# When a staged weight's conversion may begin during attention: two steps behind its load, and the late token-weight loads queued in group 5

## The chip, the core and the metric

The kernel runs on one core of a Trainium2 chip. Its time is the device time of one execution in microseconds (us), the median over runs. The core's engines work side by side, each on its own list of instructions in order: TensorE (PE in the profile; its weight loads are PEld), VectorE (DVE), ScalarE (ACT), GpSimd (POOL) and SyncE (SP), which here issues all DMA transfers.

## What is computed

Three layers follow each other, all in 32-bit precision, for 2 batches of 768 tokens with 512 features:

```python
# attention, 8 heads of 64: tokens attend only within their cluster
q_assign = argmax(q_n @ c_n);  k_assign = argmax(k_n @ c_n)
scores = scale * q @ k.T, where(q_assign == k_assign), else -1e9
attn = exp(scores - max);  out = (attn / (sum(attn) + 1e-9)) @ v
# token mixer
theta = x @ w_theta
y = w_tok_r @ (x * cos(theta)) + w_tok_i @ (x * sin(theta))
u = x + y;  x = u + relu(u @ w_ch)
# low-rank mixer and feed-forward
u = x + V.T (U.T x);  x = u + relu(u @ w_ch1) @ w_ch2
```

The weights come as 64-bit floats. Before a weight tile can be used it is converted to 32 bits and split into a high and a low part for TensorE.

## The kernel before, in words

**Stages.** `prologue` loads and packs the first heads, `attention` (L843) works through 8 groups of two heads (2 batches x 4 pairs), `mixer` does the rest. The whole order of instructions is written out by hand: what a Python call emits first stands first on its engine.

**A group of attention** has six steps, p = 0 to 5. In each step `scores_pair` (L304, L309) makes scores of the running group g on TensorE in three parts, and ScalarE their exponentials; `max_pair` (L251, L255) makes scores of the next group g+1 and VectorE three row reductions of them, so that a group has 18 reductions. After steps 2 and 5 `max_join` (L260) joins the maxima of one head, POOL splits them in two (`max_split`, L271, L272), and `max_rows` (L282 on TensorE, L285 copies on ScalarE) turns them into rows of the next group's operands. Step 5 of groups 1 to 6 ends in a *burst*: first background work is emitted, then P·V products of the whole group (L317) with `max_rows` of the next group's second head in their middle, the eviction `pv_out` (xT, L324) and the row sums (`sum_keys`, L346). In group 6 six of the twelve P·V pieces are left for group 7, which spreads them over its steps and makes no maxima.

**Operand copies.** For group g+2, `split_half` and `mask_rows` in steps 0 to 2 of group g split the raw heads and issue many small SBUF-to-SBUF copies on SyncE (L213). The value tile of group g+1 is loaded at the start of group g (`load_v`, L292).

**Weight conversion runs in the background of attention.** A `Convert` object is one tile of 128 x 768 (768 KB). Its pieces are: `load` (L390, SyncE, into one of three staging buffers `st`), `magnitude` (L399, ScalarE, out `cv`), `low` (a shift, L402, VectorE), `join` (L406, VectorE), then `hi` (L411, ScalarE, out `wh`) and `lo` (L415, POOL, out `wl`). The queues are: `conv_load` (not loaded yet), `conv_in` (loaded, at most three), `conv_do` (the pieces of the tile in hand) and `conv_after` (`hi` and `lo`). `conv_step` emits one piece. When a tile is joined, `last` emits the `magnitude` of the next tile in `conv_in` at once, whenever its load was issued:

```python
                    if conv_in:
                        conv_in[0].magnitude()
                    conv_start()
```

`fill` (L825) decides how many pieces a step gets: each step adds to a budget `owed`, 0.3 in most steps, 9.6 in the burst of groups 2 to 6, 2.5 in each step of group 7; other background items (`bg`) go first. `held[0]` is true during attention. Tiles of w_theta are queued in group 1, the first six of the token weights (wr and wi in turn, three of each) in group 2, and the other six, `late`, in group 6.

Of the kernel before, what the change touches and what calls it, by code (L numbers as in the profile page):

```python
# [25 lines left out]
NT = S // P  # L26
# [15 lines left out]
def tile_cluster_block(ctx: ExitStack, tc: tile.TileContext, qk, v, cent, wth, wr, wi, wch,  # L42
# [57 lines left out]
    def load_raw(g, i):  # L100
        t = slot(f"raw{g}_{i}")
        nc.sync.dma_start(out=t, in_=qk[g // NP, g % NP, i])
        raw[g, i] = t
# [154 lines left out]
    def max_join(g, h, eng=None):  # L258
        mx = small.tile([P, NT], F32, tag="mx", name="mx")
        nc.vector.tensor_reduce(mx, mx_t[g, h].rearrange("p (t n) -> p t n", n=2), axis=AX.X, op=ALU.max)  # L260
        mx_t[g, h] = mx
        max_split(g, h, eng or nc.gpsimd)
# [27 lines left out]
    def load_v(g):  # L290
        t = slot(f"v{g}", F32, [P, NT, P])
        nc.sync.dma_start(out=t, in_=v[g // NP, g % NP])  # L292
        v_t[g] = t
# [19 lines left out]
    def pv(g, kt, hf):  # L313
        if kt == 0 and hf == 0:
            pvt[g] = banks("pv", "pv")
        for r in range(0, P, 32):
            nc.tensor.matmul(out=pvt[g][hf][r:r + 32, :HALF], lhsT=v_t[g][:, kt, r:r + 32],  # L317
                             rhs=pt[g, r // 64, kt][:, cols(hf)],
                             start=(kt == 0), stop=(kt == NT - 1))

    def pv_out(g):
        xT[g] = slot(f"xT{g}")
        for hf in range(2):
            nc.scalar.activation(out=xT[g][:, cols(hf)], in_=pvt[g][hf][:, :HALF], func=AF.Copy)  # L324
        give("pv")
# [3 lines left out]
    def join_keys(g, h, eng):  # L329

        t = slot(f"pj{h}")
        eng.tensor_tensor(t, pt[g, h, 0], pt[g, h, 1], op=ALU.add)
        joined[g, h] = t
# [40 lines left out]
    def norm_x(g):  # L374
        nc.vector.tensor_tensor(xT[g], xT[g], rl.pop(g), op=ALU.mult)
# [42 lines left out]

    conv_load, conv_in, conv_do, conv_after = deque(), deque(), deque(), deque()
    held = [False]  # L420

    def conv_start():
        while conv_load and len(conv_in) < STAGED:
            c = conv_load.popleft()
            c.load()
            conv_in.append(c)

    def conv_step(n=1):

        for _ in range(n):  # L430
            if conv_after and not held[0]:
                conv_after.popleft()()
            if not conv_do:
                conv_start()
                if not conv_in:
                    return
                c = conv_in[0]

                def last(c=c):
                    c.join()  # L440
                    conv_in.popleft()
                    conv_after.extend([lambda f=f: f(c) for f in c.done])
                    if conv_in:
                        conv_in[0].magnitude()
                    conv_start()

                conv_do.extend((c.low, lambda: None, last))
                if c.t is None:
                    conv_do.appendleft(c.magnitude)
            conv_do.popleft()()  # L450
# [6 lines left out]
    def weigh_in(src, n, dst):  # L457
        return [Convert(src, n, i, keep_split(dst)) for i in range((n + S - 1) // S)]
# [57 lines left out]
    def split_x(b, t, eng=nc.vector):  # L516
        x = xT[b * NP + t]
        hi = slot(f"xh{t}", F32R)
        nc.scalar.activation(out=hi, in_=x, func=AF.Copy)
        lo = slot(f"xl{t}", F32R)  # L520
        eng.tensor_tensor(lo, x, f32(hi), op=ALU.subtract)
        xs[b, t] = (hi, lo)
# [320 lines left out]
    def attention():  # L843


        ORDER = [(0, 0), (0, 2), (0, 4), (1, 0), (1, 2), (1, 4)]
        BURST = (2, 5)
        pvq = deque()
        held[0] = True

        def next_pv():
            g, kt, hf = pvq.popleft()
            pv(g, kt, hf)
            if kt == NT - 1 and hf:
                pv_out(g)

        for g in range(NG):
            nxt = g + 1 < NG
            if g == 1:
                conv_load.extend(weigh_in(wth, NP * DM, wth_t))  # L860
                conv_start()
            if nxt:
                load_v(g + 1)
            if g < 2:
                bg.extend(assign.pop(g + 2))
            if g + 3 < NG:
                for i in range(2):
                    load_raw(g + 3, i)
            if g == 2:
                tok = [c for p in zip(weigh_in(wr, NT * S, wr_t), weigh_in(wi, NT * S, wi_t)) for c in p]  # L870
                conv_load.extend(tok[:6])
                conv_start()
                late = tok[6:]
            if g == 6:
                conv_load.extend(late)
                conv_start()
            if not nxt:
                for t in range(NP):
                    bg.append((1., lambda t=t: split_x(0, t, nc.gpsimd)))
            order = [(1, 0), None, (1, 2), None, (1, 4), None] if g == 0 else ORDER  # L880
            for p in range(NT):
                ready = len(pvq)
                if order[p]:
                    h, a = order[p]
                    scores_pair(g, h, a)
                    if h:
                        pvq.extend((g, kt, hf) for kt in (a, a + 1) for hf in range(2))
                if g == 0 and p < 2:
                    mask_direct(1, p, nc.scalar if p else nc.vector)
                if nxt:  # L890
                    max_pair(g + 1, p // 3, 2 * p % 6)
                    if p % 3 == 2:
                        max_join(g + 1, p // 3)

                while conv_after:
                    conv_after.popleft()()
                if p in ((1, 4) if g < 4 or not nxt else (2, 4)):
                    join_keys(g, p // 4, nc.gpsimd if g < 4 else nc.vector)
                    if 4 <= g < NG - 1 and p == 4:
                        owed[0] -= .95  # L900
                if p < 2 and g + 2 < NG:
                    split_half(g + 2, p)
                if p == (3 if g < 2 else 2) and g + 2 < NG:
                    mask_rows(g + 2)
                long = 0 < g < NG - 1 and p == 5
                if long:
                    if g + 3 < NG:
                        (_, sims), *items = assign_items(g + 3)
                        sims()
                        bg.extend(items)  # L910
                    max_rows(g + 1, 0)
                if g > 0 and p == 5:
                    bg.appendleft((.95, lambda: norm_x(g - 1)))
                    bg.appendleft((.97, lambda: spread(g - 1)))
                fill(2.5 if not nxt else .3 if p not in BURST or (g > 1 and p == 2) else 9.6 if g > 1 else 4.8)
                if not nxt:
                    for _ in range(min(ready, (2, 2, 2, 0, 4, 4)[p])):
                        next_pv()
                    if p == 5:
                        sum_keys(g, 0)  # L920
                elif long:
                    ready = len(pvq) - (6 if g == NG - 2 else 0)
                    for n in range(ready):
                        if n == ready // 2:
                            max_rows(g + 1, 1)
                        next_pv()
                    sum_keys(g, 0, NT)
                elif p == 2 and g < 2:
                    if g > 0:
                        max_rows(g, 1)  # L930
                        sum_keys(g - 1, 1)
                    for _ in range(min(ready, 6)):
                        next_pv()
                elif p == 5:
                    max_rows(g + 1, 0)
                    for _ in range(min(ready, 6)):
                        next_pv()
                    sum_keys(g, 0)
                    (_, sims), *assign[g + 3] = assign_items(g + 3)
                    sims()  # L940
                if g > 0 and p == 2:
                    row_sums(g - 1)
            while bg:
                fill(.5)
            while g and conv_after:
                conv_after.popleft()()
        held[0] = False
        while len(pvq) > 1:
            next_pv()
        nc.scalar.activation(out=warm, in_=warm, func=AF.Sin)  # L950
        next_pv()
        sum_keys(NG - 1, 1)
# [286 lines left out]
```

## Time and profile before

| | us |
|---|---|
| median of 3 runs | 675.95 |
| lowest to highest run | 675.38 to 677.36 |
| the profiled execution's own time | 675.26 |
| its span, from the first to the last instruction | 673.5 |
| TensorE busy in the span | 658.3 (98%) |
| VectorE busy | 462.3 (69%) |
| ScalarE busy | 358.3 (53%) |
| POOL busy | 313.1 (46%) |
| granted TensorE clock, mean | 0.997 of full speed |

The page sums each engine over the whole span, so that stages with different limits lie in one number. For the groups of attention one reads the table by stage (busy time of each engine in a stretch of time) and the timeline, whose rows give an instruction's start, how long it or a run of equal ones took, and in brackets how long the engine had been idle before it and what ended that. In this execution group 5 begins at 155.01 us, group 6 at 179.42, group 7 at 206.49 and the mixer at 231.45 (the first scores or theta product of each).

### The profile page before, as it was taken

To read this page: it belongs to the slowest core of one execution; us is meant where nothing else is said; L and a number is where in the kernel's file an instruction comes from. 1 tells how busy PE (TensorE), PEld (TensorE's weight loads), DVE (VectorE), ACT (ScalarE), POOL (GpSimd) and SP (SyncE) were. 2 spreads that over 40 slices of the span, in tenths; PEclk is the share of its full clock that TensorE was granted. 3 is DMA by queue.
4 is the path that set the end of the run, shared out by engine and by line. 5 is a ranking of instruction groups with operands and counts; after the bars stand their busy time and mean duration, and the time that the engine had idled before them with its cause. 6 is when DMAs were issued, how large, how long until landed. Compare 5 with 4: busy or idle time off the path is not lost.

```text
span 673.5 us, 11931 instructions
## 1 busy us (share of the span) xinstructions
PE 658.3 (98%) x4559; PEld 579.8 (86%) x4560; DVE 462.3 (69%) x795; ACT 358.3 (53%) x726; POOL 313.1 (46%) x325
## 2 busy tenths in 40 slices
PE   8899999999889999999999999999999999999998
PEld 3567777777565599999999998899999999999997
DVE  7888698797688575547375547758876576776554
ACT  8648477667388554455464445634553444543231
POOL 9445156324048532114233144967666564746221
PEclk9899999999999999999999999999999999999999
DMA  6868668766604211003101221012221222110013
GB/s 201 216 146 261 173 143 254 218 165 172 219 0 150 87 48 33 1 0 110 48 24 33 77 65 48 26 38 80 73 84 35 76 79 79 32 32 2 0 48 141
DMA packets 21786, 62.57 MB, mean 93 GB/s; under 512 B 4224, under 2 KB 7296, under 8 KB 21728
## 3 DMA queue, kind: packets, MB, share of 16 engines
q1 hardware_dynamic: 21728, 61.80, 31.7%
q8 instruction: 36, 0.59, 0.4%
q14 instruction: 22, 0.18, 0.1%
HBM read 40.35 MB, written 3.15 MB: 65 GB/s over the span
## 4 chain that ended last, share of the span: by engine, by line
PE 89%; DVE 6%; ACT 2%; DMA 1%; SPq 1%; issue 1%; POOL 0%; POOLq 0%; DVEq 0%; ACTq 0%
PE acc L810 17%; PE q L758 15%; PE y L576 15%; PE st L304 8%; PE pv L317 8%; PE h L596 5%; PE th L534 5%; PE smax L251 3%; DVE mx L255 3%; PE l L346 3%; PE g L712 3%; PE acc L731 2%; DMA st<-in_wi_dram 1%; PE sims L121 1%; PE tp L614 1%; SPq L213 1%
## 5 line engine op out<-in xcount | busy, mean ns | idle before, releaser
L810 PE MATMUL acc<-g,wh 128*128 128x384 f32 x448 | 113.6, 334 | 0.0
L772 POOL TENSOR_TENSOR g<-sum,g 128x384 fp32r<-128x384 f32 x56 | 61.9, 1107 | 83.4 <-ACT g L771 83.4
L255 DVE TENSOR_REDUCE mx<-smax 128x1 f32<-128x512 f32 x144 | 89.1, 680 | 14.5 <-PE smax L251 14.5
L766 DVE TENSOR_TENSOR xT<-acc,xT 128x384 f32<-128x384 f32 x112 | 61.9, 555 | 46.3 <-PE acc L810 46.2
L309 ACT ACTIVATE p<-st 128x512 f32<-128x512 f32 x192 | 80.2, 530 | 25.1 <-PE st L304 24.6
L576 PE MATMUL y<-wh,z 128*128 128x384 f32 x384 | 87.6, 340 | 0.3 <-ACT z L554 0.3
L304 PE MATMUL st<-qp,kp 128*128 128x256 f32 (+1 forms) x384 | 79.4, 348 | 2.4 <-ACT p L309 1.5
L810 PEld LDWEIGHTS acc<-g,wh 128*128 128x128 f32 x448 | 80.7, 188 | 0.1
L415 POOL TENSOR_TENSOR wl<-cv,wh 128x768 fp32r<-128x768 f32 (+1 forms) x31 | 56.2, 1819 | 49.2 <-ACT wh L411 35.4
L810 PE MATMUL acc<-g,wl 128*128 128x384 f32 x224 | 74.8, 334 | 0.0
L304 PEld LDWEIGHTS st<-qp,kp 128*128 128x128 f32 x384 | 57.8, 191 | 19.5 <-issue 7.2
L770 ACT ACTIVATE sum<-sum 128x384 f32<-128x384 f32 x56 | 29.3, 523 | 82.3 <-DVE sum L766 82.3
L766 DVE TENSOR_TENSOR sum<-q,sum 128x384 f32<-128x384 f32 x98 | 53.0, 553 | 24.3 <-PE q L758 20.8
L576 PEld LDWEIGHTS y<-wh,z 128*128 128x128 f32 x384 | 66.9, 188 | 0.5 <-ACT z L554 0.5
L317 PE MATMUL pv<-p,v 128*32 128x384 f32 x768 | 66.6, 487 | 0.0
L560 POOL TENSOR_TENSOR z<-tht,z 128x256 fp32r<-128x256 f32 x24 | 18.2, 756 | 91.7 <-ACT z L554 91.6
L317 PEld LDWEIGHTS pv<-p,v 128*32 128x32 f32 x768 | 38.9, 110 | 18.7 <-issue 8.2
L406 DVE SCALAR_TENSOR_TENSOR cv<-cv,st 128x768 int32<-128x768 int32 (+3 forms) x47 | 49.5, 1054 | 0.8
L251 PE MATMUL smax<-kp,qp 128*128 128x512 f32 x192 | 44.6, 349 | 4.6 <-ACT qp L285 2.0
L576 PE MATMUL y<-wl,z 128*128 128x384 f32 x192 | 48.8, 335 | 0.0
L251 PEld LDWEIGHTS smax<-kp,qp 128*128 128x128 f32 x192 | 32.8, 191 | 15.3 <-issue 4.3
L193 POOL TENSOR_TENSOR lo<-raw,hi 128x768 fp32r<-128x768 f32 x16 | 29.3, 1838 | 35.4 <-ACT hi L188 24.2
(177 smaller groups left out, 1440.8 us busy)
## 6 DMA issues: line engine op xcount, KB each, us to landing
st<-in_w_dram SPq DMA_DIRECT2D x17, 512.0 KB, 3.6
st<-in_w_dram SPq DMA_DIRECT2D x10, 768.0 KB, 4.2
raw<-in_qk_dram SPq DMA_DIRECT2D x16, 384.0 KB, 5.0
qp<-hi SPq DMA_DIRECT2D x26, 192.0 KB, 3.1
st<-in_wr_dram SPq DMA_DIRECT2D x6, 768.0 KB, 4.3
st<-in_wi_dram SPq DMA_DIRECT2D x6, 768.0 KB, 5.8
kp<-hi SPq DMA_DIRECT2D x32, 96.0 KB, 3.1
qp<-lo SPq DMA_DIRECT2D x32, 96.0 KB, 2.7
```

Source lines behind the costliest of these rows:

```text
L251: nc.tensor.matmul(out=ps[:, c:c + w], lhsT=qp[s, h, 0][:, (a + j) * P:(a + j + 1) * P], rhs=kp[s, h, 0][:, k0:k0 + w], start=True, stop=True)
L255: nc.vector.tensor_reduce(mx_t[g, h][:, o:o + n], ps.rearrange("p (n w) -> p n w", n=n), axis=AX.X, op=ALU.max)
L304: nc.tensor.matmul(out=ps[:, c:c + n], lhsT=kp[s, h, w][:, (a + j) * P:(a + j + 1) * P], rhs=qp[s, h, w][:, q0:q0 + n], start=(w == 0), st ...
L309: nc.scalar.activation(out=pt[g, h, a + j][:, q0:q0 + n], in_=ps[:, c:c + n], func=AF.Exp, scale=float(D) ** -0.5)
L317: nc.tensor.matmul(out=pvt[g][hf][r:r + 32, :HALF], lhsT=v_t[g][:, kt, r:r + 32], rhs=pt[g, r // 64, kt][:, cols(hf)], start=(kt == 0), st ...
L406: nc.vector.scalar_tensor_tensor(t, t, 3, self.lw, op0=ALU.logical_shift_left, op1=ALU.bitwise_or)
L415: nc.gpsimd.tensor_tensor(t[:, :c.w], c.t, f32(c.hi[:, :c.w]), op=ALU.subtract)
L576: nc.tensor.matmul(out=yps[u, j][hf][:, :HALF], lhsT=lhs, rhs=w[st][e][:, hf * HALF:(hf + 1) * HALF], start=(st == 0 and n == 0), stop=(st ...
L758: nc.tensor.matmul(out=ps[:, :HALF], lhsT=w[a][:, j * P:(j + 1) * P], rhs=u_block(self.b, y, e, j), start=(n == 0), stop=(n == 5))
L766: nc.vector.tensor_tensor(out, ps[:, :HALF], x, op=ALU.add)
L772: nc.gpsimd.tensor_tensor(t[:, 1], r, f32(t[:, 0]), op=ALU.subtract)
L810: nc.tensor.matmul(out=ps[:, :HALF], lhsT=wv[a], rhs=self.g[i, hf][:, x], start=(m == 0), stop=(m == 5))
```

## The change

A counter `clock` holds the number of the running attention step, 6g + p. A load notes it. During attention a tile's `magnitude` may only be emitted when at least two steps have passed since its load was emitted, both in `last`, where the next tile's `magnitude` follows a join, and in `conv_step`, where a new tile is taken in hand. After attention nothing is asked. And the six late tiles are queued at the start of group 5 instead of group 6.

```diff
+    clock = [0]
+
+    def landed(c):
+
+        return not held[0] or clock[0] - c.at > 1
...
             c = conv_load.popleft()
             c.load()
+            c.at = clock[0]
             conv_in.append(c)
...
-                if not conv_in:
+                if not conv_in or not (conv_in[0].t is not None or landed(conv_in[0])):
                     return
...
-                    if conv_in:
+                    if conv_in and landed(conv_in[0]):
                         conv_in[0].magnitude()
...
-            if g == 6:
+            if g == 5:
                 conv_load.extend(late)
                 conv_start()
...
                 ready = len(pvq)
+                clock[0] = NT * g + p
```

What it moves is seen in the engines' orders. On ScalarE, at the end of group 5 and the first steps of group 6 (qp<-mrow are the copies of the maxima, cv<-st a `magnitude`, xT the eviction, wh a `hi`, p<-st the exponentials), before:

```order
L285 ACTIVATE qp_86<-mrow 2x384 x2
L399 ACTIVATE cv<-st 128x768 x3
L285 ACTIVATE qp_90<-mrow 2x384 x2
L324 ACTIVATE xT_2511<-pv 128x384 x2
L411 ACTIVATE wh<-cv 128x768 x3
L309 ACTIVATE p_2555<-st 128x512
```

and after:

```order
L285 ACTIVATE qp_86<-mrow 2x384 x2
L399 ACTIVATE cv<-st 128x768 x2
L285 ACTIVATE qp_90<-mrow 2x384 x2
L324 ACTIVATE xT_2513<-pv 128x384 x2
L411 ACTIVATE wh<-cv 128x768 x3
...
L309 ACTIVATE p_2582<-st 128x512
L399 ACTIVATE cv<-st 128x768
L309 ACTIVATE p_2610<-st 128x512
```

The third `magnitude` of the burst (the third tile of wi) now stands behind the exponentials of step 1 of group 6. In group 7 the pieces of the fourth wi tile and those behind it stand up to a step later; its three `magnitude` and three `hi` stay within the group.

On VectorE, among the reductions of group 6's steps 0 to 2 (mx<-smax) and in its burst (rb and xT<-xT,rb are the normalisation, st<-st a `low`, cv<-cv,st a `join`), before:

```order
L255 TENSOR_REDUCE mx_2572<-smax 128x1
L402 TENSOR_SCALAR st<-st 128x768
L255 TENSOR_REDUCE mx_2572<-smax 128x1
L255 TENSOR_REDUCE mx_2572<-smax 128x2
...
L371 STREAM_TRANSPOSE rb<-rl 128x768
L375 TENSOR_TENSOR xT_2511<-xT_2511,rb 128x768
L406 SCALAR_TENSOR_TENSOR cv<-cv,st 128x768
```

and after:

```order
L255 TENSOR_REDUCE mx_2570<-smax 128x1 x2
L255 TENSOR_REDUCE mx_2570<-smax 128x2
...
L371 STREAM_TRANSPOSE rb<-rl 128x768
L375 TENSOR_TENSOR xT_2513<-xT_2513,rb 128x768
L402 TENSOR_SCALAR st<-st 128x768
L406 SCALAR_TENSOR_TENSOR cv<-cv,st 128x768
```

The `low` has left the reductions and stands in the burst, directly ahead of its `join`.

On SyncE, behind the last operand copies for group 7 (kp<-oh), before:

```order
L213 DMA kp_99<-oh 16x384
L390 DMA st<-in_wi_dram 128x1536
L292 DMA v_2549<-in_v_dram 128x768
L390 DMA st<-in_wr_dram 128x1536
L390 DMA st<-in_wi_dram 128x1536
```

and after:

```order
L213 DMA kp_99<-oh 16x384
L390 DMA st<-in_wi_dram 128x1536
L390 DMA st<-in_wr_dram 128x1536
L390 DMA st<-in_wi_dram 128x1536
L292 DMA v_2551<-in_v_dram 128x768
```

The value tile of group 7 has moved behind the fourth tiles of wr and wi. TensorE's order is the same in both.

## Rows read from the trace of the kernel before

**Rows 1.** The page, part 1: engine, busy us, share of the span, instructions
```profile
PE 658.3 (98%) x4559; PEld 579.8 (86%) x4560; DVE 462.3 (69%) x795; ACT 358.3 (53%) x726; POOL 313.1 (46%) x325
```
**Rows 2.** Table by stage, groups 5, 6, 7: stretch, length, busy us, clock, DMA
```profile
155.01:179.42 24.41, 24.41 (x221) 18.08 (x222) 19.54 (x33) 14.36 (x31) 6.67 (x14) 1.00 0.64 166
179.42:206.49 27.07, 22.24 (x173) 15.22 (x173) 20.92 (x32) 19.81 (x40) 10.81 (x17) 1.00 0.27 102
206.49:231.45 24.96, 24.96 (x234) 12.43 (x233) 18.13 (x15) 20.01 (x40) 20.48 (x16) 1.00 0.41 130
```
**Rows 3.** Timeline, SyncE's queue: start us, us, engine line operation tiles
```profile
175.63 0.53 SPq L390 DMA_DIRECT2D st<-in_wi_dram  x1
176.26 0.38 SPq L292 DMA_DIRECT2D v<-in_v_dram  x1
176.73 0.38 SPq L390 DMA_DIRECT2D st<-in_wr_dram  x1
177.21 0.50 SPq L390 DMA_DIRECT2D st<-in_wi_dram  x1
```
**Rows 4.** Chain of waits (start, us, what); line 390's landings, 150 to 225 us
```profile
175.63 5.49 DMA st<-in_wi_dram
...
DMA to landing us min/median/max: 4.2/4.4/8.9
```
**Rows 5.** Timeline, ScalarE, groups 5 and 6
```profile
157.94 1.66 ACT L309 ACTIVATE p<-st 128x512 f32<-128x512 f32 x4
...
169.35 1.79 ACT L399 ACTIVATE cv<-st 128x768 f32<-128x768 f32 x2
181.21 0.89 ACT L399 ACTIVATE cv<-st 128x768 f32<-128x768 f32 x1 [10.07 <-DMA st<-in_wi_dram]
182.12 0.97 ACT L285 ACTIVATE qp<-mrow 2x384 fp32r<-2x384 f32 x2
```
**Rows 6.** Timeline, TensorE, groups 5 and 6
```profile
167.96 0.23 PE L282 MATMUL mrow<-identb,m 128*2 128x128 bf16 x2
...
183.14 1.01 PE L251 MATMUL smax<-kp,qp 128*128 128x256 f32 x3 [1.98 <-ACT qp L285]
...
186.72 0.73 PE L304 MATMUL st<-qp,kp 128*128 128x512 f32 x2 [1.48 <-ACT p L309]
...
197.46 0.23 PE L282 MATMUL mrow<-identb,m 128*2 128x128 bf16 x2
...
200.99 0.27 PE L282 MATMUL mrow<-identb,m 128*2 128x128 bf16 x3 [1.26 <-POOL m L272]
```
**Rows 7.** Timeline, VectorE: reductions and last joins of groups 5 and 6
```profile
156.86 1.89 DVE L255 TENSOR_REDUCE mx<-smax 128x1 f32<-128x512 f32 x3 [1.22 <-PE smax L251]
...
170.64 0.17 DVE L260 TENSOR_REDUCE mx<-mx 128x6 f32<-128x12 f32 x1
...
181.20 0.69 DVE L255 TENSOR_REDUCE mx<-smax 128x1 f32<-128x512 f32 x1 [1.22 <-PE smax L251]
183.68 1.29 DVE L255 TENSOR_REDUCE mx<-smax 128x2 f32<-128x512 f32 x2 [1.79 <-PE smax L251]
187.81 1.89 DVE L255 TENSOR_REDUCE mx<-smax 128x1 f32<-128x512 f32 x3 [2.84 <-PE smax L251]
189.62 1.02 DVE L402 TENSOR_SCALAR st<-st 128x768 int32<-128x768 int32 x1
...
200.13 0.17 DVE L260 TENSOR_REDUCE mx<-mx 128x6 f32<-128x12 f32 x1
```
**Rows 8.** Timeline, the burst of group 6 and what follows: VectorE, ScalarE
```profile
202.96 0.57 DVE L402 TENSOR_SCALAR st<-st 128x768 int32<-128x768 int32 x1
...
207.20 1.64 ACT L309 ACTIVATE p<-st 128x512 f32<-128x512 f32 x4 [1.67 <-PE st L304]
```
**Rows 9.** Timeline, end of group 7: last exponentials, P·V that reads them
```profile
222.20 1.81 ACT L309 ACTIVATE p<-st 128x512 f32<-128x512 f32 x4
...
226.75 2.76 PE L317 MATMUL pv<-p,v 128*32 128x384 f32 x32
```

## The prediction

> **What bounds the kernel now.** I read the page first: TensorE is busy for 658.3 of 673.5 us [rows 1], so only a place where it stands still, or works at another engine's pace, can give time. Then the table by stage, cut at the starts of the attention groups [rows 2]. Group 5 takes 24.41 us with TensorE busy throughout. Group 6 takes 27.07 us with TensorE busy for 22.24, although its program holds less TensorE work than group 5's (half of the P·V products of its end are left for the last group). Group 7 has no idle time again. So the change can gain in group 6.
>
> The timeline shows the cause. In the burst at the end of group 5 ScalarE converts three staged weights in a row, ahead of the copies of the second row of maxima. The first two run at 169.35 us; the third, the third tile of wi, waits 10.07 us for its transfer [rows 5]. SyncE has issued that transfer only at 175.63 us, because the operand copies of group 7 stand ahead of it [rows 3], and it lands 5.49 us later [rows 4]. Behind the waiting conversion stand, on ScalarE, the two copies of maxima (182.12 us), the eviction of xT, three weight splits and the exponentials of group 6. TensorE goes on with P·V and row sums, which need nothing from ScalarE, and then stands: 1.98 us until the copies of maxima free a bank, 1.48 us for an exponential, and 1.26 us later for the split of the maxima on POOL [rows 6].
>
> The third of these waits is the one that sets the price. VectorE must make 18 row maxima in a group; their join, POOL's split and the second row of maxima on TensorE end the group. In group 5 this runs from 156.86 to 170.81 us (the last join starts at 170.64 and takes 0.17), 13.95 us. In group 6 it runs from 181.20 to 200.30 us, 19.10 us: VectorE stands 1.79 and 2.84 us because TensorE delivers no products, and a weight's shift (1.02 us at 189.62) lies between the maxima [rows 7].
>
> **The change, part by part.**
>
> *The rule of two steps.* Only one conversion is put off: the third of wi, loaded in step 5 of group 5, may begin in step 1 of group 6. It leaves ScalarE's queue in the burst and comes back behind the exponentials of step 1. No instruction is added or lost. I take the wait of 10.07 us as gone. What does that give?
> - By TensorE's own idle rows, 1.98 + 1.48 = 3.46 us: the lower value.
> - By VectorE's chain, 19.10 − 13.95 = 5.15 us. The check: the waits 1.79 + 2.84 = 4.63 and the shift of 1.02 make 5.65; group 5's chain has some half a microsecond of short waits of its own, which come back.
>
> I take 5.15, because the chain also ends last after the change: the first maximum stays at 181.20 us (its product is out before the stall), so the last join ends at 181.20 + 13.95 = 195.15 us. TensorE reaches the first row of maxima 12.95 us after the group's start in group 5 (167.96 − 155.01), thus at 179.42 + 12.95 = 192.37 us here, and has P·V for 2.27 us (in group 6 from 197.46 to 200.99 − 1.26 = 199.73) [rows 6]: it is ready at 194.6 us and waits for VectorE and POOL once more. So the 1.26 us stays, about as long, and all that the chain gains TensorE gains. From the last join to group 7's first scores it takes 206.49 − 200.30 = 6.19 us as before; group 7 begins at 201.3 instead of 206.49 us.
>
> *The conversion in step 1 of group 6.* ScalarE spends 0.9 us more there (181.21 took 0.89 [rows 5]). In group 5 a split of the same size lies behind the exponentials of steps 0 and 1 and costs TensorE nothing, so I cost it at nothing. Its cover is ScalarE's idle time: 14.36 of 24.41 us busy in group 5 [rows 2].
>
> *The shift of wi's low bits* leaves VectorE's maxima and stands in the burst of group 6 behind the normalisation. There a shift costs 0.57 us alone [rows 8]. The two weight splits on ScalarE behind it come 0.6 us later; ScalarE has 1.67 us in hand before the exponentials of group 7 [rows 8]. Cost nothing; without that cover 0.6 us.
>
> *The late loads, one group earlier.* Without them the queue holds the same transfers; with them wr's and wi's fourth tiles are issued directly behind the third wi, and the value tile of group 7 goes behind both. On SyncE that moves it from 176.26 to about 177.2 us [rows 3]; it is read from 206 us on, or 201 after the gain, and lands long before. The fourth wi waits for a staging buffer whose join runs in the same burst. The next load behind these is only issued in the burst of group 6. Cost nothing.
>
> *The last group.* Steps 1 to 5 there hold three conversions and three weight splits on ScalarE; these now begin in step 2. Total work is the same (20.01 of 24.96 us busy [rows 2]). The step that loses is 5: two more pieces of about 1 us stand ahead of its exponentials in steps 3 and 4, while step 2 lost two, so I estimate them 1.1 us late. They end at 222.20 + 1.81 = 224.0 us before; P·V that reads them begins at 226.75 us [rows 9]. 1.1 is under 2.7. Cost nothing; bound, if ScalarE were late by all six pieces of about 1 us, 6 − 2.7 = 3.3 us.
>
> **Sum.** 675.26 (the profiled execution) − 5.15 = 670.1 us. That execution lies 0.7 us below the median of the three runs, 675.95; I state the forecast for the median: 675.95 − 5.15 = **670.8 us**.
>
> **Rivals.**
> - *A. Only the visible idle goes*, 3.46 us: 672.5. It would be so if VectorE's chain in group 6 is slow by itself and not by the stall. For it: the chain also bounds after the change, and POOL's three weight splits now run earlier, beside it. Against it: the rows of group 5, with the same 18 maxima and no stall, and VectorE's two waits named as waits for TensorE [rows 7].
> - *B. The wait moves to step 1 of group 6*, so the change does not do what it says. The rule counts steps of the program, not landings, and the load is issued by SyncE long after its place in the program. The step's exponentials end in group 5 at 159.43 us or 4.42 us after the group's start (157.94 + 1.66, less the overlap of 0.17) [rows 5]; in group 6 that is 183.8 us. The transfer landed at 181.1 us, so it has 2.7 us in hand. The same three transfers follow it, but now the two of 768 KB stand ahead of the value tile of 384 KB. If it shares evenly with the next two, 5.49 × 2304/1920 = 6.6 us (768 KB three times against 768, 384 and 768), landing at 182.2, still in time; with the longest landing of this line, 8.9 us [rows 4], at 184.5, a wait of 0.7 us: 671.5 at most, as the banks hold products for more than that. The Trainium skill, DMA: Bandwidth & Descriptors, section Queues, rings and completion order, states that each engine takes descriptors in ring order, so what is queued behind a transfer would not slow it. By that rule alone B would have no chance; the landing of 5.49 us beside a median of 4.4 [rows 4] speaks against trusting it.
> - *C. Slower than before*, by B's mechanism at a larger size: ScalarE stands in step 1, where no burst of P·V covers TensorE. Each microsecond beyond 183.8 then costs up to one; the gain of 5.15 is used up and another 2.03 lost once the tile lands after 191.0 us, which is 15.4 us after its issue. No landing of this line comes near. Time from there: over 678.0.
> - *D. The last group gives it back*, by up to 3.3 us from ScalarE's lateness: 672 to 674.1.
> - *E. No change*, 676: group 7's start is held by something that the trace does not show as last, such as the operand copies. Against it: these are issued before 175.6 us.
>
> **How the numbers follow.** 0.3% of 675.95 is 2.03 us, about what a measurement can tell from no change. Forecast (gain of 4.3 to 5.7) 0.72; A 0.14; B 0.05; D 0.04; E 0.03; C 0.02. The first four are faster by more than 2.03: 0.95; E is the same: 0.03; C slower: 0.02. The range reaches at the low end to a gain of 5.65 from the profiled execution, 669.6, less 0.2 for scatter: 669.4. At the high end it takes in A and B, 672.5, and half a microsecond of scatter: 673.0. The forecast, A and B hold 0.91 of the chance; scatter and misjudged terms take the rest down to 0.8.
>
> **What would show it.** In the profile after, ScalarE's wait for wi's transfer is gone or under 1 us; TensorE's two waits of 1.98 and 1.48 us are gone and one of about 1.2 us for POOL's split stays; the last join of group 6 ends at about 195.2 us, 13.9 to 14.0 after the first maximum; group 6 takes about 21.9 us and group 7 about 25.0. The forecast is wrong if group 6 keeps over 23.5 us, if a wait for a transfer appears behind the exponentials of its step 1, or if group 7 or the stage after it grows by more than a microsecond.

## The result and the profile after

The changed kernel takes 670.93 us (median of 6 runs, 670.34 to 672.43); the kernel before, run beside it, 676.83 us (6 runs, 675.38 to 678.64). The ratio is 0.9915, with a 95% interval of 0.9896 to 0.9935: faster by some 5.8 us (the medians differ by 5.90). The forecast was 670.8 us, and its gain 5.15. The profiled execution took 670.64 us, its span 668.9.

The table by stage, cut where the groups begin in this trace (stretch, length, busy us of PE, PEld, DVE, ACT, POOL, then clock and DMA), for groups 5, 6, 7:

```profile
155.60:179.94 24.34, 24.34 (x221) 18.02 (x221) 19.52 (x32) 18.50 (x38) 8.52 (x16) 1.00 0.64 167
179.94:201.93 21.99, 20.73 (x173) 15.26 (x173) 19.96 (x32) 15.89 (x33) 8.36 (x15) 1.00 0.31 115
201.93:226.87 24.94, 24.94 (x233) 12.45 (x233) 17.18 (x15) 20.17 (x40) 20.98 (x17) 1.00 0.42 139
```

One cut of [rows 2] has to be set right first. In all of these stretches the cut lies 0.07 us behind the row with the group's first scores; only group 6 of the kernel before was cut 0.14 us behind its row. Cut like the others, at 179.35, groups 5 and 6 of the kernel before read:

```profile
179.28 1.66 PE L304 MATMUL st<-qp,kp 128*128 128x512 f32 x8
...
206.42 1.68 PE L304 MATMUL st<-qp,kp 128*128 128x512 f32 x8
```

```profile
155.01:179.35 24.34, 24.34 (x221) 18.01 (x221) 19.52 (x32) 14.36 (x31) 6.67 (x14) 1.00 0.64 165
179.35:206.49 27.14, 22.31 (x173) 15.29 (x173) 20.93 (x32) 19.81 (x40) 10.81 (x17) 1.00 0.27 103
```

So group 6 fell from 27.14 to 21.99 us, by 5.15; the groups beside it moved by 0.02 us at most. The mixer takes the rest of the span, 668.9 − 226.87 = 442.03 us against 673.5 − 231.45 = 442.05 before. So the whole difference of the two traces lies in group 6, but for 0.6 us by which this execution began group 5 later (155.60 against 155.01).

ScalarE in the timeline, burst of group 5 and first steps of group 6, answers to [rows 5]:

```profile
169.94 1.79 ACT L399 ACTIVATE cv<-st 128x768 f32<-128x768 f32 x2
172.88 0.97 ACT L285 ACTIVATE qp<-mrow 2x384 fp32r<-2x384 f32 x2 [1.15 <-PE mrow L282]
...
182.72 1.64 ACT L309 ACTIVATE p<-st 128x512 f32<-128x512 f32 x4 [0.44 <-PE st L304]
184.22 0.91 ACT L399 ACTIVATE cv<-st 128x768 f32<-128x768 f32 x1
185.00 1.67 ACT L309 ACTIVATE p<-st 128x512 f32<-128x512 f32 x4
```

Two conversions run in the burst, and the copies of the maxima follow as soon as TensorE has their product. The third conversion runs at 184.22 us, with no idle time before it. VectorE and TensorE answer to [rows 7] and [rows 6]:

```profile
181.79 1.89 DVE L255 TENSOR_REDUCE mx<-smax 128x1 f32<-128x512 f32 x3 [1.22 <-PE smax L251]
...
195.57 0.17 DVE L260 TENSOR_REDUCE mx<-mx 128x6 f32<-128x12 f32 x1
```

```profile
192.90 0.23 PE L282 MATMUL mrow<-identb,m 128*2 128x128 bf16 x2
...
196.43 0.27 PE L282 MATMUL mrow<-identb,m 128*2 128x128 bf16 x3 [1.25 <-POOL m L272]
```

From the first maximum to the end of the last join VectorE's chain takes 195.57 + 0.17 − 181.79 = 13.95 us, the time of group 5 before, in place of 19.10. TensorE's waits of 1.98 and 1.48 us are gone; the one for POOL's split is still there, 1.25 against 1.26 us. And SyncE's queue, answering to [rows 3]:

```profile
176.25 0.53 SPq L390 DMA_DIRECT2D st<-in_wi_dram  x1
176.87 0.38 SPq L390 DMA_DIRECT2D st<-in_wr_dram  x1
177.34 0.38 SPq L390 DMA_DIRECT2D st<-in_wi_dram  x1
177.82 0.93 SPq L292 DMA_DIRECT2D v<-in_v_dram  x1
```

### The profile page after: what moved, and what is told of

It is laid out like the page before. It is cut to its first block, busy times and chain, and to the rows that moved or that the text cites. A ratio compares the mean times of both kernels' runs of the same rounds, so it can differ in the third digit from the quotient of the medians.

```text
span 668.9 us, 11928 instructions
## 1 busy us (share of the span) xinstructions
PE 657.9 (98%) x4559; PEld 580.5 (87%) x4560; DVE 460.8 (69%) x795; ACT 358.9 (54%) x726; POOL 313.1 (47%) x325
## 4 chain that ended last, share of the span: by engine, by line
PE 92%; DVE 5%; ACT 2%; DMA 1%; issue 0%; SPq 0%; POOL 0%; POOLq 0%; DVEq 0%
PE acc L816 17%; PE q L764 15%; PE y L582 15%; PE st L304 9%; PE pv L317 9%; PE h L602 5%; PE th L540 5%; PE smax L251 4%; PE l L346 4%; DVE mx L255 3%; PE g L718 3%; PE acc L737 3%; PE tp L620 1%; PE th L544 1%; PE sims L121 1%; DMA raw<-in_qk_dram 1%
```

## The experiments

The theories. **S**: ScalarE's wait of 10 us for one transfer is the cause, and SyncE's queue the reason for it. **V**: VectorE's chain sets the end of group 6, so a delay is priced by what it does to that chain. Rivals: **A**, only the visible idle time of TensorE counts; **Q**, the earlier loads bring the gain. The length of group 6 is read from each run's table by stage.

| kernel | group 6, us | ratio to before (95% interval) |
|---|---|---|
| before | 27.14 | 1 |
| changed | 21.99 | 0.9915 (0.9896 to 0.9935) |
| loads alone | 27.13 | 1.000 (0.9984 to 1.0016) |
| rule alone | 21.99 | 0.9936 (0.9918 to 0.9954) |
| rule alone, again | 22.00 | 0.993 (0.9913 to 0.9947) |
| changed, again | 21.99 | 0.9916 (0.9901 to 0.993) |
| changed, shift back | 22.49 | 0.9933 (0.9916 to 0.995) |
| before, shift moved | 26.53 | 1.0001 (0.9988 to 1.0014) |
| changed, wait without cover | 22.51 | 0.994 (0.9918 to 0.9961) |
| before, early load | 22.56 | 0.9965 (0.9952 to 0.9978) |
| changed, additions on POOL | 20.60 | 0.9914 (0.9897 to 0.9931) |
| the same, shifts of groups 3 and 4 early | 20.61 | 0.9894 (0.9873 to 0.9915) |

**The two parts of the change, each alone.** The loads without the rule:

```diff
-            if g == 6:
+            if g == 5:
                 conv_load.extend(late)
```

> The kernel before with the second part of the change alone: the late tiles queued in group 5, no rule of two steps. Theory S (the stall): the third conversion of wi still stands in the burst, ScalarE waits about 10 us for its transfer, group 6 takes 27.0 to 27.2 us and the time is that of before, ratio 1.00. Theory Q (the earlier loads bring the gain): group 6 near 22 us, ratio 0.992. In both the value tile of group 7 lands about 8.8 us after its issue, as in the changed kernel, and nobody waits for it.

Its median is 676.31 us (before 675.89) and its group 6 takes 27.13 us. ScalarE waits as before, in the timeline:

```profile
182.04 0.89 ACT L399 ACTIVATE cv<-st 128x768 f32<-128x768 f32 x1 [10.06 <-DMA st<-in_wi_dram]
```

So the loads by themselves gain nothing. The rule without the loads (the changed kernel with `g == 6` again), run twice, the second time beside the changed kernel:

> The changed kernel with its second part undone: the late tiles are queued in group 6 again, the rule of two steps stays. Theory S: all of the gain is the rule's; group 6 takes 22.0 us and ratio and time are those of the changed kernel, 0.991 to 0.993, 670 to 671.5 us. The value tile of group 7 lands about 5.8 us after its issue again instead of 8.8. Theory Q: without the earlier loads the gain is gone or smaller, group 6 over 23 us.

> The rule of two steps alone once more (late tiles queued in group 6), on the same chip as the changed kernel. Its first run had equal attention groups and a later stage 1.9 us longer, behind gaps between POOL instructions. If these gaps have nothing to do with the change, they appear in some executions of any kernel: the medians of the two agree within 1 us and group 6 takes 22.0 us in both. If the order of the loads matters by itself, this one stays 1 us or more above the changed kernel.

> The changed kernel itself once more, beside the next one on the same chip. Group 6 takes 22.0 us, ratio 0.991 to 0.994.

Group 6 takes 21.99 and 22.00 us, that of the changed kernel run beside it 21.99. So the gain in group 6 is the rule's, and Q falls. The medians are 672.22 and 671.96 us. The first lies above what was expected (670 to 671.5). The second lies 1.15 us above the changed kernel on the same chip (670.81), with ranges that overlap (669.27 to 672.83 against 669.98 to 671.09); a microsecond or more was to be the sign that the order of the loads matters by itself. Their profiles place the difference outside group 6. In the first, the mixer is 1.9 us longer, and the chain of waits has gaps between POOL's instructions there:

```profile
430.60 1.81 POOL wl L415
432.41 3.64 issue
436.05 0.04 POOLq L481
436.09 1.01 POOL g L778
```

In the second the time is lost before group 0 begins (its first scores at 22.18 us, against 20.45 beside it), where the two programs are still the same; groups 1 to 5 are equally long, and group 6 begins 1.6 us later (181.73 against 180.10). So the loss in that execution cannot come from the order of the loads. Whether the order makes the gaps of the first likelier, and so is worth up to a microsecond of the median, stays open.

**The late load.** In the kernel before, two pieces of conversion more are emitted at the start of group 5. One is a join that frees a staging buffer, so the third wi tile's load comes ahead of the operand copies. Its conversion stays in the burst, which now holds two in place of three:

```diff
+            if g == 5:
+                conv_step(2)
             if g < 2:
                 bg.extend(assign.pop(g + 2))
```

> The kernel before, without the rule and with the late tiles in group 6, but with two pieces of conversion more at the start of group 5, so that a staging buffer comes free and the load of the third wi tile is issued ahead of group 7's operand copies. The third conversion stays in the burst of group 5. Theory S with its cause in SyncE's queue: the load is issued near 157 us and landed before 165, ScalarE does not wait, TensorE's waits of 1.98 and 1.48 us are gone though no rule holds the conversion back. A join now stands among the maxima of group 6 (0.95 us), so theory V gives a chain of 14.4 to 14.9 us and group 6 22.4 to 23.0 us; time 671 to 672. If the place of the conversion in the burst were itself the cause, group 6 would stay near 27 us and the time near 676.

The load is issued at 156.96 us, lands after 4.4 us, and ScalarE has no wait for a transfer. Group 6 takes 22.56 us without any rule, its chain 14.52 (182.82 to 197.34). So the place of the conversion was harmless; the lateness of its load was not.

The lateness has two sources, and S named only one of them. The first row is from the kernel before, the others from this run:

```profile
172.60 0.95 DVE L406 SCALAR_TENSOR_TENSOR cv<-cv,st 128x768 int32<-128x768 int32 x1
```

```profile
156.01 0.92 DVE L406 SCALAR_TENSOR_TENSOR cv<-cv,st 128x768 int32<-128x768 int32 x1
156.96 0.33 SPq L390 DMA_DIRECT2D st<-in_wi_dram  x1
```

The load fills the buffer that this join reads. Before, the join ended at 173.55 us and the load was issued 2.08 us later, behind the copies; here it was issued 0.03 us after the join. So by these rows the copies account for some 2 of the 10 us, an estimate; the rest is the late join and the 5.49 us of the transfer. The edit moved the join and the place in the queue together, and no run moves the copies alone.

The time is 673.79 us, more than expected: group 5 grew from 24.34 to 25.49 us, its chain from 13.95 to 15.08. VectorE's timeline there shows why, with POOL's behind it:

```profile
159.41 1.89 DVE L255 TENSOR_REDUCE mx<-smax 128x1 f32<-128x512 f32 x3 [0.21 <-PE smax L251]
161.21 1.52 DVE L402 TENSOR_SCALAR st<-st 128x768 int32<-128x768 int32 x1
```

```profile
160.46 3.97 POOL L193 TENSOR_TENSOR lo<-raw,hi 128x768 fp32r<-128x768 f32 x2
```

The two pieces moved a shift into the maxima of group 5, where POOL splits raw heads; it took 1.52 us there instead of 0.56. I had not priced that. The two groups together gain 3.4 us, the medians 2.1; the difference is not placed.

**The price is VectorE's chain.** Two runs move the same shift, once in each direction.

```diff
 # changed kernel, step 2 of group 6
+                if (g, p) == (6, 2):
...
+                    conv_do.popleft()()
+                    conv_do.appendleft(lambda: None)
```

> The changed kernel with one instruction put back: the shift of the third wi tile stands again among VectorE's maxima of group 6 (step 2), not in the burst. Theory V (VectorE's chain sets the end of group 6): the chain from the first maximum to the end of the last join grows from 13.95 by about 0.5 us to 14.4, TensorE's wait for POOL's split grows from 1.25 to about 1.7 us, group 6 takes 22.4 to 22.5 us instead of 21.99. Theory A (only TensorE's two visible waits behind the stall counted): nothing moves, 21.99 us. The time itself, 0.5 us of 671, cannot tell them apart; the stage can.

```diff
 # kernel before, conv_step
+            if conv_do[0] == conv_in[0].low and held[0] and clock[0] == 6 * NT + 1:
+                return
             conv_do.popleft()()
...
+                clock[0] = NT * g + p
```

> The kernel before, with ScalarE's wait of 10 us left in place, and only the shift of the third wi tile taken from the maxima of group 6 to its burst. Theory V counts the two terms apart: the waits of 1.79 and 2.84 us for TensorE stay, the shift goes, short waits of some 0.2 to 0.4 us come back; the chain takes 18.3 to 18.6 us instead of 19.10, group 6 26.3 to 26.6 us instead of 27.07, time down by 0.5 to 0.8. Theory A: the shift costs nothing, group 6 stays at 27.07.

With the shift back, the chain runs from 182.30 to 196.72 us (14.42), and group 6 takes 22.49 us, as V says and A does not:

```profile
182.30 1.89 DVE L255 TENSOR_REDUCE mx<-smax 128x1 f32<-128x512 f32 x3 [1.24 <-PE smax L251]
...
189.35 0.55 DVE L402 TENSOR_SCALAR st<-st 128x768 int32<-128x768 int32 x1
...
196.55 0.17 DVE L260 TENSOR_REDUCE mx<-mx 128x6 f32<-128x12 f32 x1
```

One part of the expectation missed: TensorE's wait for POOL's split did not grow to 1.7 us.

```profile
193.88 0.23 PE L282 MATMUL mrow<-identb,m 128*2 128x128 bf16 x2
...
197.41 0.27 PE L282 MATMUL mrow<-identb,m 128*2 128x128 bf16 x3 [1.26 <-POOL m L272]
```

TensorE came to its first row of maxima 13.46 us after the group's start (193.88 − 180.42), not 12.96 (192.90 − 179.94). It had been slowed earlier: the scores for the maxima of step 4 took 1.11 us at 190.25, in place of 0.85 at 189.74, and that time is counted as busy: 21.14 us against 20.73. That they waited for VectorE to empty a bank is argued, not shown.

With the stall left in and the shift taken out of the maxima, group 6 takes 26.53 us, 0.61 less. The two waits of the chain stay, the first of them shorter, and one short wait comes back:

```profile
185.63 1.29 DVE L255 TENSOR_REDUCE mx<-smax 128x2 f32<-128x512 f32 x2 [1.55 <-PE smax L251]
189.75 1.89 DVE L255 TENSOR_REDUCE mx<-smax 128x1 f32<-128x512 f32 x3 [2.84 <-PE smax L251]
192.11 1.89 DVE L255 TENSOR_REDUCE mx<-smax 128x1 f32<-128x512 f32 x3 [0.47 <-PE smax L251]
...
201.70 0.17 DVE L260 TENSOR_REDUCE mx<-mx 128x6 f32<-128x12 f32 x1
```

The chain takes 18.49 us (183.38 to 201.87), also 0.61 less than 19.10. Not all of it is the shift's. The transfer landed after 5.2 us here and ScalarE waited 9.82 us, so that VectorE's first wait was 1.55 in place of 1.79. From the end of the second wait the chain takes 12.12 us (189.75 to 201.87) against 12.49 before (187.81 to 200.30): the shift is worth 0.37. The time, 676.33 against 676.60 us, cannot show half a microsecond.

**A wait without cover.** The third conversion stands between the burst and group 6's first exponentials:

```diff
 # changed kernel, end of a group
+            if g == 5:
+                conv_in[0].magnitude()
+                conv_do.append(lambda: None)
```

> The changed kernel with the conversion of the third wi tile put at the end of group 5, behind the burst and ahead of all exponentials of group 6, where no P.V products cover TensorE. The tile lands about 5.3 us after its issue, so ScalarE waits some 2 us there and the first exponentials come about 1.9 us later than 1.0 us after the group's start. This prices rival C. If each microsecond of such a wait costs TensorE one, group 6 takes 23.5 to 24 us and the time is 672.5 to 673. If the free banks cover it, group 6 stays at 22.0 to 22.4 us. I expect something between: TensorE waits 0.5 to 1.5 us for a bank in step 0 or 1 and group 6 takes 22.4 to 23.4 us.

```profile
181.59 0.90 ACT L399 ACTIVATE cv<-st 128x768 f32<-128x768 f32 x1 [2.17 <-DMA st<-in_wi_dram]
182.40 4.68 ACT L309 ACTIVATE p<-st 128x512 f32<-128x512 f32 x12
```

ScalarE waits 2.17 us and then makes the exponentials of three steps in one go. Group 6 grows by 0.52 us (22.51 − 21.99): VectorE's short waits for products of steps 1 and 2 rise to 0.45 and 0.44 us from 0.21 and 0.20. I had expected TensorE to wait for a bank; it has no such idle row, but its busy time grew from 20.73 to 21.25 us. So a microsecond of such a wait cost a quarter of one here; that free banks covered the rest is argued, not shown. The time, 671.95 us, is within the spread of the changed kernel's runs.

**Taking work from the chain.** If VectorE's chain bounds, giving some of it away must gain again. Here the two additions of exponentials of group 6 go to POOL.

```diff
-                    join_keys(g, p // 4, nc.gpsimd if g < 4 else nc.vector)
+                    join_keys(g, p // 4, nc.gpsimd if g < 4 or g == 6 else nc.vector)
```

> The changed kernel with the two additions of exponentials of group 6 (pj, 0.95 us each on VectorE) given to POOL. Theory V: VectorE's chain loses up to 1.74 us and no longer ends last; TensorE's wait of 1.25 us for POOL's split goes, and with it some 0.2 us of slower scores in step 5: group 6 takes 20.5 to 20.8 us, the time falls to about 669.6. Theory A: no change, 21.99 us. Rival P: POOL takes about 1.85 us for each and its split of the maxima comes late by that: group 6 stays at 21.5 to 22.5 us.

Group 6 takes 20.60 us and the median is 669.71 us. The chain takes 12.62 us (181.45 to 194.07) and TensorE's wait for POOL's split is gone:

```profile
181.45 1.88 DVE L255 TENSOR_REDUCE mx<-smax 128x1 f32<-128x512 f32 x3 [1.24 <-PE smax L251]
...
193.90 0.17 DVE L260 TENSOR_REDUCE mx<-mx 128x6 f32<-128x12 f32 x1
```

```profile
194.67 0.27 PE L282 MATMUL mrow<-identb,m 128*2 128x128 bf16 x3
```

POOL took 1.84 and 1.83 us for the two additions, but its split of the maxima was not late: it still waited 0.44 us for VectorE's join. Rival P falls. TensorE is now busy for 20.47 of the 20.60 us, so the chain no longer ends last. The gain is shown in the stage alone; the ratio, 0.9914, is that of the changed kernel.

The same view on groups 3 and 4, with the shift emitted ahead of the first maximum:

```diff
 # end of a group, on top of the last edit
+            if g in (2, 3):
+                conv_step()
+                conv_do.appendleft(lambda: None)
```

> The changed kernel with the additions of group 6 on POOL (as in the earlier run) and, in groups 3 and 4 too, the shift taken out of VectorE's maxima: it is emitted ahead of the group's first maximum, where VectorE waits 1.2 us for TensorE anyway. Theory V, carried to other groups: group 3 falls from 25.28 to 24.7 to 24.9 us, group 4 from 25.56 to 25.1 to 25.2 us, group 6 stays at 20.6; time 668.6 to 669.2, under that of the earlier run by 0.7 to 1.0. If only group 6 is paced by VectorE, groups 3 and 4 stay as they are.

```profile
104.70:129.47 24.77, 24.77 (x229) 19.29 (x229) 21.38 (x36) 17.56 (x37) 13.18 (x19) 1.00 0.77 211
129.47:154.53 25.06, 25.06 (x230) 19.18 (x229) 21.48 (x37) 16.29 (x35) 9.51 (x16) 1.00 0.75 221
178.92:199.53 20.61, 20.48 (x174) 15.37 (x173) 18.20 (x30) 15.92 (x33) 11.06 (x17) 1.00 0.32 122
```

Groups 3 and 4 took 25.28 and 25.56 us before; here 24.77 and 25.06, 0.5 us less each. Their chains, from the first maximum to the end of the last join, fell as much: from 13.19 to 12.69 us (106.58 to 119.27) and from 14.40 to 13.92 (131.33 to 145.25). TensorE's idle time there had been 0.10 and 0.13 us, so A could not give this. The median, 668.46 us (ratio 0.9894), is the lowest of the study; its interval overlaps that of the run above.

## Why the prediction was right

**The sum.** The gain of 5.15 us came as 5.15 in the profile (27.14 − 21.99, both cut alike; [rows 2], which I worked from, give 27.07). The step that carried it, that VectorE's chain returns to group 5's 13.95 us and still ends last, is met to the hundredth (13.95), and so is the 1.25 us left for POOL's split. Group 6 was said to take 21.9 and group 7 25.0; they take 21.99 and 24.94. Four runs show that group 6 follows the chain and that this is no coincidence. With the additions on POOL, the shift moved, the shift put back and the wait without cover, the chain changed by −1.33, −0.61, +0.47 and +0.48 us, and group 6 by −1.39, −0.61, +0.50 and +0.52. That the median came within 0.13 us of the forecast is in part luck: in six runs the kernel before stood at 676.83 us, 0.88 above the median that the sum began from, and the medians differ by 5.90.

**Why the transfer was late** was only half right. The prediction put it on the operand copies ahead in SyncE's queue. They held the load for 2.08 us (173.55 to 175.63); until then its buffer was in use. The forecast does not rest on this, since the rule takes the wait away whatever makes it.

**Rival A**, the 3.46 us of visible idle time, failed for the reason given against it. TensorE's idle time in group 6 fell by 3.57 us (4.83 to 1.26), and its busy time from 22.31 to 20.73: 1.58 us of the gain had been counted as busy.

**Rivals B and C.** The third wi tile landed 5.3 us after its issue at 176.25 us, thus near 181.5, and its conversion began at 184.22: 2.7 us in hand, as read from the trace before, where I had feared 1.6. My estimate of 6.6 us, by an even share of three transfers, was the wrong one. The landings of the transfers issued at 176.25 and 177.82 us:

```profile
DMA to landing us min/median/max: 5.3/5.3/5.3
...
DMA to landing us min/median/max: 8.8/8.8/8.8
```

The first is wi's, the second the value tile's, which took 5.8 us when it stood second in the queue. What is queued later landed later; what stood first was not slowed by it. The Trainium skill, DMA: Bandwidth & Descriptors, section Queues, rings and completion order, states that each engine takes descriptors in ring order. The trace agrees: the first transfer took 5.3 us with two of 768 KB directly behind it, and 5.5 with 384 KB and 768 KB. I had trusted that rule too little. Why the first took 5.3 to 5.5 us, where the early load of the experiment above took 4.4, is not shown; the copies just ahead of it are one candidate. C's price of up to one microsecond for each of ScalarE's was too high for a short wait: a quarter, measured over 2.17 us; a long one was not tried.

**The terms costed at nothing** held. The conversion in step 1 costs group 6 nothing that can be seen: its chain equals group 5's. Its cover was read from the wrong figure: ScalarE's 14.36 us in group 5 were low because the stall had pushed work into group 6 (18.50 after the change). In group 6 after it is 15.89 of 21.99. The shift in the burst took 0.55 us at 197.53, and ScalarE still had 1.12 us in hand before group 7's exponentials (1.67 before). The late loads change neither group 6 nor 7.

**The last group** was mis-sized in the cautious direction. I had its last exponentials 1.1 us late; they began 15.71 us after the group's start before (222.20 − 206.49) and 15.93 after:

```profile
217.86 1.74 ACT L309 ACTIVATE p<-st 128x512 f32<-128x512 f32 x4
...
222.17 2.76 PE L317 MATMUL pv<-p,v 128*32 128x384 f32 x32
```

They are 0.2 us late and end 2.6 us before P·V needs them. The estimate gave little credit for the two pieces that step 2 lost; no run tests this. Rival D had nothing to give back, and with group 7 starting earlier by all of the chain's gain E falls too.

## What to carry to other kernels

Price a stall by the chain that ends the stage, not by the idle rows of the busiest engine: compare the same chain in a neighbouring stage without the stall, since an engine that works at another's pace counts as busy. An instruction that waits for a transfer holds up all that stands behind it on its engine; look in the issuing queue, and at what frees the buffer that it fills, for why the transfer is late, and either issue it earlier or let the waiting instruction stand where it arrives anyway. A rule that counts program steps knows nothing of landings: here the load stood in step 5, was issued 2.1 us after its buffer came free, and landed 2.7 us ahead of its use in step 1.

## What the runs showed of the hardware that I had not expected

The same shift of 128 x 768 took 0.55 us on VectorE alone, 1.02 in the kernel before while POOL made weight splits, 1.52 beside POOL's split of raw heads and 2.2 in the bursts of group 6 beside weight splits (2.19 at 200.92 us in the run with the shift put back), while the maxima beside it kept their 0.63 us each. That POOL's work is the cause is read from the overlap in time; no run tests it alone. A cheap instruction in a chain is to be priced with what POOL does at that moment.

Executions of one kernel spread by 2 to 4 us (670.34 to 672.43 after, 674.70 to 678.51 before on one chip), and the traces show it outside the change: group 6 began between 179.4 and 181.7 us in kernels whose groups 1 to 5 are equally long, and one execution lost 1.9 us in the mixer beside gaps between POOL's instructions. Half a microsecond is seen in a stage of a trace long before it is seen in a median.
